# Two pairs of heads to a PSUM bank in half of the value products, some scores a slot later, left-over queries in other banks, and keys transposed without zeros

## The chip, the cores and the metric

The program runs on one core of one Trainium2 chip. The metric is the device time of one execution in microseconds, lower is better; the median of the runs is quoted. All matrix work is on TensorE (PE), with VectorE (DVE), ScalarE (ACT) and GpSimd (POOL) around it; SyncE (SP) issues the DMAs.

## What is computed

```python
# q, k, v: (8 batches, 8 heads, 576 tokens, 64)
k_p = k.reshape(B, H, 72, 8, D).mean(axis=3)      # keys and values pooled by 8
v_p = v.reshape(B, H, 72, 8, D).mean(axis=3)
attn = softmax(q @ k_p.T / 8)                     # 72 keys per head
x = (attn @ v_p) -> rows of 512                   # 4608 x 512
# first MLP
h = x @ w_in                                      # 512 -> 1024
solu = h * softmax(h); ln = layernorm(solu) * g_ln
x = ln @ w_out                                    # 1024 -> 512
# second MLP
out = ((x @ w1) * (x @ w2)) @ w3 @ w_out2
```

## The kernel before

The program has three stages. In the first (0 to about 565 us of the trace) attention and the first MLP run together, in the second (to about 690 us) the MLP goes on while the weights of the second MLP are prepared, and the third is the second MLP alone. The change touches only the first stage.

**Groups and units.** The tokens of a batch are cut into two groups of the attention: the even group has 256 tokens (two tiles of 128), the odd one has 256 and the 64 left over, as a third tile `t = 2`. There are 16 groups `a` (names carry the number: `sc8_1_0` are scores of group 8, tile 1, first four heads). The first MLP works on units of 256 rows, one behind the attention by two groups.

**The order.** PE and SP execute in the order in which the code is written, and the code is driven by a table of slots: `put(slot, fn)` hangs a step on a slot, and each slot ends with a piece of the first MLP, either a quarter of 128 rows through `w_in` (kind h: six matmuls `h` of 512 columns) or a quarter of a column block through `w_out` (kind x or y: twelve matmuls `x` of 256 columns). A unit has 16 slots: hhhh xxxx hhhh yyyy. ACT, DVE and POOL are put in order by a list scheduler when the program is built, each engine then executes its list strictly in that order.

**Attention by steps** (`Group`): `pq` transposes 128 queries (four 128x128 transposes, ACT copies them to `qT`); `sc` makes scores in two banks of four heads each; `exp` takes the maxima (`mx`, DVE) and eight exponentials (`ea`, ACT); `normalize` scales them (`sm` DVE, `pr` POOL); `pt` transposes the probabilities (and `px` those of the left-over keys); ACT and DVE split them into high and low words; `av` multiplies them with the pooled values, five matmuls for each of the four pairs of heads, and ACT (`xh`) and DVE (`xl`) split the result into the input of the MLP. In odd groups DVE also copies the 64 left-over rows (`X`). The distances of these steps in slots are in `GAPS`.

**Keys** (`Batch`): `pool_k` sums eight tokens on DVE (`kp`), ACT copies the sums into a tile `KBD` that has zeros for the other head of a pair, `transpose_k` transposes `KBD` (`pkm`) and a masked tile `KLB` of the left-over keys (`pkl`), and ACT and DVE copy both to `bdt`, which has the keys of a pair of heads side by side with zeros between. The first batch pools with matmuls instead (`pool_k_first`).

**Banks.** PSUM has eight banks: three of tag `ba` (function `bank`) for the attention, three of tag `bm` (`bankm`) for `px`, `lt` (transposes of the normalised rows) and the outputs of `w_out`, two as one pair for `h`. A new tile must wait until the last reader of the bank's tile before it has read it.

**SP.** `store` sends the first MLP's output (`xo`, copied by ACT) to DRAM; that issue waits for `xo`, and the loads behind it on SP wait with it.

Of the kernel before, what the change touches and what calls it, by code (L numbers as in the profile page):

```python
# [18 lines left out]
def attention_moe_kernel(  # L19
# [25 lines left out]
    nc = tc.nc  # L45
# [218 lines left out]
    nc.gpsimd.memset(KBD, 0.0)  # L264
# [6 lines left out]
    KLB = A1.tile([P, H, D], F32, tag="KLB", name="KLB")  # L271
    nc.gpsimd.memset(QL, 0.0)
    nc.gpsimd.memset(KLB, 0.0)
# [12 lines left out]
    class Batch:  # L286


        def __init__(self, b):
            self.b = b  # L290
            self.k, self.v = [None, None], [None, None]

        def load_main(self, src, to, i):
            t = A.tile([P, 2, POOL * D], F32, tag="kvn", name=f"kv{self.b}_{i}")
            for hh in range(2):
                nc.sync.dma_start(
                    t[64 * hh : 64 * hh + 64],
                    src[self.b, 4 * i + hh : 4 * i + hh + 3 : 2, 0:512, :].rearrange("h (k e) d -> k h (e d)", e=POOL),
                )
            to[i] = t  # L300

        def load_left(self, src, copies):
            t = A.tile([P, POOL * D], F32, tag="kvl", name=f"kvl{self.b}", bufs=1)
# [4 lines left out]
            return t  # L308

        def load_k(self, i):  # L310
            self.load_main(k, self.k, i)

        def load_kl(self):
            self.kl = self.load_left(k, 1)

        def load_v(self, i):
            self.load_main(v, self.v, i)

        def load_vl(self):
            self.vn = self.load_left(v, 2)  # L320

        def pool_k(self, i):
            kp = A.tile([P, 2, D], F32, tag="kp", name=f"kp{self.b}_{i}", bufs=1)
            nc.vector.tensor_reduce(kp, self.k[i].rearrange("p c (e d) -> p c d e", e=POOL), axis=AX.X, op=ALU.add)
            for hh in range(2):
                r = slice(64 * hh, 64 * hh + 64)
                nc.scalar.activation(KBD[r, 2 * i : 2 * i + 2, hh, :], kp[r], AF.Copy)

        def pool_k_first(self, i):

            if i == 0:
                self.pm = bank(f"pkm{self.b}")
                self.bdt = A.tile([P, NP, 2, KP], F32, tag="bdt", name=f"bdt{self.b}")
                nc.gpsimd.memset(self.bdt, 0.0)
            for c in range(2):
                for a in range(2):
                    r, o = slice(D * a, D * a + D), (2 * i + c) * P + D * a
                    for e in range(POOL):
                        s_ = self.k[i][:, c, e * D : e * D + D]
                        nc.tensor.matmul(  # L340
                            self.pm[r, o : o + D], s_, ident[:, r], start=(e == 0), stop=(e == POOL - 1)
                        )

        def pool_kl(self):
            tree(self.kl[0:64], D)
            nc.gpsimd.tensor_tensor(KLB[0:64], heads(self.kl[0:64, 0:D], 64), head_mask(64), ALU.mult)

        def transpose_k(self):
            if self.b == 0:
                bdt, pm = self.bdt, self.pm.rearrange("p (c a k) -> p c a k", c=NP, a=2)  # L350
                for a in range(2):
                    r = slice(D * a, D * a + D)
                    nc.scalar.activation(bdt[r, :, a, 0:KM], pm[r, :, a, :], AF.Copy)
            else:
                bdt = self.bdt = A.tile([P, NP, 2, KP], F32, tag="bdt", name=f"bdt{self.b}")
                pm = bank(f"pkm{self.b}")
                for p in range(NP):
                    nc.tensor.transpose(pm[:, p * P : p * P + P], KBD[:, p].rearrange("p a d -> p (a d)"), ident)
                nc.scalar.activation(bdt[:, :, :, 0:KM], pm.rearrange("p (c a k) -> p c a k", c=NP, a=2), AF.Copy)
            pl = bank(f"pkl{self.b}")  # L360
            for p in range(NP):
                nc.tensor.transpose(
                    pl[:, p * P : p * P + P], KLB[:, 2 * p : 2 * p + 2].rearrange("p a d -> p (a d)"), ident
                )

            def left():
                for p in range(NP):
                    nc.vector.tensor_copy(
                        bdt[:, p, :, KM:KP],
                        pl[:, p * P + 16 * p : p * P + 16 * p + 16].rearrange("p (a k) -> p a k", a=2),  # L370
# [24 lines left out]
    class Group:  # L395
# [20 lines left out]
        def pq(self, t):  # L416
            n, nm = P, f"{self.a}_{t}"
            pq = bank("pq" + nm)
# [102 lines left out]
        def av(self, i):  # L521
# [4 lines left out]
            for p in (2 * i, 2 * i + 1):  # L526
                av = bank(f"av{self.a}_{p}")
# [10 lines left out]
                for i, (l, r) in enumerate(terms):  # L538
                    nc.tensor.matmul(av[:, 0:w], l, r, start=(i == 0), stop=(i == 4))  # L539
                split(x[0][:, p], x[1][:, p], av[:, 0:U])  # L540
                if self.g == 1:
# [98 lines left out]
    GAPS = [(1, 2, 4, 3)] + [(1, 3, 2, 5)] * (2 * B - 1)  # L640
# [24 lines left out]
    for a in range(NG):  # L665
# [399 lines left out]
```

## Time and profile before

| | us |
|---|---|
| median of 3 runs | 1323.86 |
| fastest of the runs | 1323.69 |
| the profiled execution | 1323.81 |
| its span, first to last instruction | 1322.0 |
| PE busy | 1239.4 (94%) |
| DVE busy | 825.8 (62%) |
| ACT busy | 534.0 (40%) |
| POOL busy | 422.6 (32%) |

The profiled execution stands within 0.05 us of the median, so times of the trace and of the runs can be set side by side; 1.81 us lie around the span. A busy PE is not PE at its peak, since matmuls are pipelined; what PE waits for is read from the rows that name a releaser. The rows that matter come below.

### The profile page before, as it was taken

To read this page: it belongs to the slowest core of one execution; us is meant where nothing else is said; L and a number is where in the kernel's file an instruction comes from. 1 tells how busy PE (TensorE), PEld (TensorE's weight loads), DVE (VectorE), ACT (ScalarE), POOL (GpSimd) and SP (SyncE) were. 2 spreads that over 40 slices of the span, in tenths; PEclk is the share of its full clock that TensorE was granted. 3 is DMA by queue.
4 is the path that set the end of the run, shared out by engine and by line. 5 is a ranking of instruction groups with operands and counts; after the bars stand their busy time and mean duration, and the time that the engine had idled before them with its cause. 6 is when DMAs were issued, how large, how long until landed. Compare 5 with 4: busy or idle time off the path is not lost.

```text
span 1322.0 us, 21967 instructions
## 1 busy us (share of the span) xinstructions
PE 1239.4 (94%) x8284; PEld 1125.3 (85%) x8284; DVE 825.8 (62%) x1629; ACT 534.0 (40%) x1515; POOL 422.6 (32%) x509
## 2 busy tenths in 40 slices
PE   7778989989998999999999999999999999999992
PEld 5467889888888888998988899999999999999992
DVE  6889877677777777645357555546454645454541
ACT  4565656666665656554354221212121212121210
POOL 4452534342524434220000141524243333334220
PEclk9889999999999999999999999999999999999997
DMA  9533536454544364313133101010101101010000
GB/s 230 140 104 101 153 98 164 116 160 128 159 112 118 116 160 120 100 59 136 39 113 126 32 2 64 1 64 1 65 31 35 58 7 65 1 64 1 33 1 32
DMA packets 85698, 109.43 MB, mean 83 GB/s; under 512 B 43608, under 2 KB 43608, under 8 KB 85592
## 3 DMA queue, kind: packets, MB, share of 16 engines
q1 hardware_dynamic: 85592, 108.03, 28.7%
q8 instruction: 65, 1.06, 0.3%
q14 instruction: 41, 0.34, 0.1%
HBM read 78.65 MB, written 29.36 MB: 82 GB/s over the span
## 4 chain that ended last, share of the span: by engine, by line
PE 74%; DVE 11%; DMA 6%; ACT 4%; issue 3%; SPq 1%; POOL 0%; ACTq 0%; DVEq 0%; POOLq 0%
PE p L925 9%; PE p L927 9%; PE p L926 9%; PE h L567 8%; PE acc L971 5%; PE acc L974 5%; PE acc L973 5%; DMA f<-in_moe_w_dram 4%; PE x L625 4%; PE x L624 4%; PE x L626 4%; PE av L539 2%; PE lt L610 2%; PE sc L436 2%; DVE cvb L180 1%
## 5 line engine op out<-in xcount | busy, mean ns | idle before, releaser
L945 POOL TENSOR_TENSOR a<-a,b 128x256 f32<-128x256 f32 x72 | 52.9, 735 | 477.5 <-DVE b L944 350.9
L929 ACT ACTIVATE p<-p 128x256 f32<-128x256 f32 x72 | 27.9, 387 | 397.6 <-PE p L927 365.7
L624 PE MATMUL x<-lnh,gwh 128*128 128x256 f32 x576 | 167.3, 290 | 0.0
L625 PE MATMUL x<-lnl,gwh 128*128 128x256 f32 x576 | 163.8, 284 | 2.6 <-DVE lnl L614 2.6
L626 PE MATMUL x<-lnh,gwl 128*128 128x256 f32 x576 | 163.4, 284 | 0.0
L189 POOL TENSOR_TENSOR cvb<-cvb,cvm 128x512 f32<-128x512 f32 x46 | 60.0, 1305 | 180.7 <-DVE cvm L182 148.6
L625 PEld LDWEIGHTS x<-lnl,gwh 128*128 128x128 f32 x576 | 110.8, 192 | 4.2 <-DVE lnl L614 3.2
L457 ACT ACTIVATE ea<-sc,mx 128x72 f32<-128x72 f32 x320 | 98.3, 329 | 36.9 <-DVE mx L454 36.8
L974 PE MATMUL acc<-wfl,ph 128*128 128x512 f32 x288 | 113.1, 393 | 0.0
L973 PE MATMUL acc<-wfh,ph 128*128 128x512 f32 x288 | 112.9, 392 | 0.0
L624 PEld LDWEIGHTS x<-lnh,gwh 128*128 128x128 f32 x576 | 110.6, 192 | 1.2 <-DVE lnl L614 0.2
L626 PEld LDWEIGHTS x<-lnh,gwl 128*128 128x128 f32 x576 | 110.6, 192 | 0.0
L944 DVE TENSOR_TENSOR b<-b,p 128x256 f32<-128x256 f32 x72 | 30.2, 419 | 122.9 <-PE p L927 122.9
L567 PE MATMUL h<-winh,xh 128*128 128x512 f32 x288 | 100.4, 430 | 0.0
L567 PE MATMUL h<-winl,xh 128*128 128x512 f32 x288 | 91.4, 399 | 0.0
L567 PE MATMUL h<-winh,xl 128*128 128x512 f32 x288 | 90.4, 395 | 0.0
L925 PE MATMUL p<-th,w1h 128*128 128x256 f32 x288 | 81.6, 283 | 1.1 <-ACT p L929 1.1
L971 PE MATMUL acc<-wfh,pl 128*128 128x512 f32 x288 | 82.5, 393 | 0.0
L614 DVE TENSOR_TENSOR lnl<-lt,lnh 128x512 fp32r<-128x512 f32 x72 | 49.2, 686 | 52.7 <-ACT lnh L613 52.1
L926 PE MATMUL p<-th,w1h 128*128 128x256 f32 x288 | 81.5, 283 | 0.0
L927 PE MATMUL p<-th,w1l 128*128 128x256 f32 x288 | 81.5, 283 | 0.0
L933 DVE TENSOR_TENSOR u<-p,p 128x256 f32<-128x256 f32 x72 | 30.3, 422 | 77.3 <-PE p L927 76.2
(196 smaller groups left out, 3766.9 us busy)
## 6 DMA issues: line engine op xcount, KB each, us to landing
f<-in_moe_w_dram SPq DMA_DIRECT2D x32, 512.0 KB, 6.2
x2d<-xo SPq DMA_DIRECT2D x36, 256.0 KB, 2.0
xq<-x2d SPq DMA_DIRECT2D x36, 256.0 KB, 2.7
out_dram<-ot SPq DMA_DIRECT2D x36, 256.0 KB, 2.5
kv<-in_k_dram SPq DMA_DIRECT2D x32, 256.0 KB, 3.6
q<-in_q_dram SPq DMA_DIRECT2D x32, 256.0 KB, 8.3
kv<-in_v_dram SPq DMA_DIRECT2D x32, 256.0 KB, 3.7
f<-in_moe_w_out_dram SPq DMA_DIRECT2D x16, 512.0 KB, 6.1
```

The costliest lines, as they stand in the source:

```text
L189: self.engine.tensor_tensor(self.f, self.f, self.m.bitcast(F32), ALU.add)
L457: nc.scalar.activation(e[0:n, x], half[a][:, h], AF.Exp, bias=mx[0:n, x : x + 1], scale=1.0, accum_out=sm[0:n, x : x + 1],)
L567: nc.tensor.matmul(self.ph[:, a], s_[:, c], w_[:, c, a * 512 : a * 512 + 512], start=first, stop=last)
L624: nc.tensor.matmul(o, gw[0][:, f, ws], self.th[:, f], start=(f == 0), stop=False)
L625: nc.tensor.matmul(o, gw[0][:, f, ws], self.tl[:, f], start=False, stop=False)
L626: nc.tensor.matmul(o, gw[1][:, f, ws], self.th[:, f], start=False, stop=(f == FC - 1))
L925: nc.tensor.matmul(o, wh[:, c, fsl], th[:, c], start=c == 0, stop=False)
L926: nc.tensor.matmul(o, wh[:, c, fsl], tl[:, c], start=False, stop=False)
L927: nc.tensor.matmul(o, wl[:, c, fsl], th[:, c], start=False, stop=c == 1)
L971: nc.tensor.matmul(accs[t], pl[:, ts], wh, start=False, stop=(fc == FC - 1))
L973: nc.tensor.matmul(accs[t], ph[:, ts], wh, start=(fc == 0), stop=False)
L974: nc.tensor.matmul(accs[t], ph[:, ts], wl, start=False, stop=False)
```

## The change

1. Value products of an even group: two pairs of heads go into the two halves of one bank, so a group takes two banks and not four, and ACT and DVE split 512 columns at a time, not 256. Odd groups (320 columns a pair) stay as they were.
2. The scores of tile 1 of an even group (from group 2 on) are put one slot later, and the gap from its `pt` to `av` is one slot shorter, so `av` stays where it was.
3. The transposed left-over queries (`pq` of tile 2) take a bank of tag `bm`, not `ba`.
4. Keys are loaded so that the two heads of a pair lie side by side. The pooled tile `kp` (now two buffers) is transposed as it is, two transposes a batch and not four, and ACT copies the two halves to two `bdt` tiles that are set to zero once. `KBD` and its copies on ACT are gone. The left-over keys are summed twice into one tile `KL8` (four POOL additions, no multiplication by the mask), one transpose and not four, and two DVE copies and not four. The first batch's pooling has 32 matmuls of 128 columns, not 64 of 64 columns.

```diff
-    KBD = A1.tile([P, NP, 2, D], F32, tag="KBD", name="KBD")
+    BDT = [A1.tile([P, NP, 2, KP], F32, tag=f"bdt{i}", name=f"bdt{i}") for i in range(2)]
...
+    KL8 = A1.tile([P, POOL * D], F32, tag="KL8", name="KL8")
...
         def load_k(self, i):
-            self.load_main(k, self.k, i)
+
+            self.load_main(k, self.k, i, lambda h, r: slice(h + 2 * r, h + 2 * r + 2))
...
         def pool_k(self, i):
-            kp = A.tile([P, 2, D], F32, tag="kp", name=f"kp{self.b}_{i}", bufs=1)
+            kp = self.kp[i] = A.tile([P, 2, D], F32, tag="kp", name=f"kp{self.b}_{i}")
             nc.vector.tensor_reduce(kp, self.k[i].rearrange("p c (e d) -> p c d e", e=POOL), axis=AX.X, op=ALU.add)
-            for hh in range(2):
-                r = slice(64 * hh, 64 * hh + 64)
-                nc.scalar.activation(KBD[r, 2 * i : 2 * i + 2, hh, :], kp[r], AF.Copy)
...
         def transpose_k(self):
...
+            if self.b:
+                self.pm = bank(f"pkm{self.b}")
+                for i in range(2):
+                    nc.tensor.transpose(
+                        self.pm[:, i * P : i * P + P], self.kp[i].rearrange("p a d -> p (a d)"), ident
+                    )
...
+            pl = bank(f"pkl{self.b}")[:, 0:P]
+            nc.tensor.transpose(pl, KL8[:, 2 * D : 4 * D], ident)
+            pl = pl[:, 0:64]
+            for a in range(2):
+                r = slice(D * a, D * a + D)
+                nc.scalar.activation(bdt[r, :, a, 0:KM], pm[r], AF.Copy)
...
-            pq = bank("pq" + nm)
+            pq = (bank if t < 2 else bankm)("pq" + nm)
...
             for p in (2 * i, 2 * i + 1):
-                av = bank(f"av{self.a}_{p}")
+                if self.g or p % 2 == 0:
+                    av_bank = bank(f"av{self.a}_{p}")
+                av = av_bank if self.g else av_bank[:, p % 2 * U : p % 2 * U + U]
...
-                split(x[0][:, p], x[1][:, p], av[:, 0:U])
-                if self.g == 1:
+                for n, (l, r) in enumerate(terms):
+                    nc.tensor.matmul(av[:, 0:w], l, r, start=(n == 0), stop=(n == 4))
+                if self.g == 0 and p % 2:
+                    ps = slice(p - 1, p + 1)
+                    split(x[0][:, ps], x[1][:, ps], av_bank.rearrange("p (c n) -> p c n", c=2))
+                elif self.g == 1:
+                    split(x[0][:, p], x[1][:, p], av[:, 0:U])
...
-    GAPS = [(1, 2, 4, 3)] + [(1, 3, 2, 5)] * (2 * B - 1)
+    GAPS = [(1, 2, 4, 3)] + [(1, 3, 2, 5 - (a % 2 == 0)) for a in range(1, 2 * B)]
...
-            put(base + 2 + 4 * t, grp.sc, t)
+            put(base + 2 + 4 * t + (a > 0 and a % 2 == 0 and t == 1), grp.sc, t)
```

Three places show what moves. The first is on PE after the value products of group 7 (`av7_3` is their last pair), where the scores of group 8, tile 1 (`sc8_1_0`, `sc8_1_1`) stand; `x2_5_1` is an output block of the first MLP. Before:

```order
L539 MATMUL av7_3_3397<-ptx7_3029,vlh3_2646 128x320
L539 MATMUL av7_3_3397<-ptx7_3029,VLL_111 128x320
L436 MATMUL sc8_1_0_3412<-bdt4_3183,qT8_1_3344 128x144 x2
L436 MATMUL sc8_1_1_3415<-bdt4_3183,qT8_1_3344 128x144 x2
L624 MATMUL x2_5_1_3421<-lnh5_3080,gwh_103 128x256
L625 MATMUL x2_5_1_3421<-lnl5_3081,gwh_103 128x256
```

and now, where twelve `x` matmuls stand between `av7_3` and these rows:

```order
L634 MATMUL x2_5_1_3305<-lnl5_2978,gwh_103 128x256
L635 MATMUL x2_5_1_3305<-lnh5_2977,gwl_104 128x256
L440 MATMUL sc8_1_0_3321<-bdt0_105,qT8_1_3234 128x144 x2
L440 MATMUL sc8_1_1_3324<-bdt0_105,qT8_1_3234 128x144 x2
L633 MATMUL x2_5_1_3305<-lnh5_2977,gwh_103 128x256
L634 MATMUL x2_5_1_3305<-lnl5_2978,gwh_103 128x256
```

The scores moved behind one slot of `x`. In the built program the bank of `av7_3`, which nothing needed for long before, is then the next one taken: by `pt8_0`, one slot of `x` after the scores.

The second place is DVE's list around the value products of group 8 (`xl8` splits them, `kp5_0` pools keys of batch 5, `mx9_0` are maxima of group 9; `cvm` and `cvb` belong to the conversion of a weight). Before:

```order
L180 SCALAR_TENSOR_TENSOR cvb_3778<-f64_3647,cvb_3778 128x512
L324 TENSOR_REDUCE kp5_0_3803<-kv5_0_3684 128x128
L101 TENSOR_TENSOR xl8_3667<-av8_0_3668,xh8_3666 128x256
L101 TENSOR_TENSOR xl8_3667<-av8_1_3676,xh8_3666 128x256
L181 TENSOR_SCALAR cvm_3777<-cvb_3778 128x512
L182 SCALAR_TENSOR_TENSOR cvm_3777<-f64_3647,cvm_3777 128x512
L101 TENSOR_TENSOR xl8_3667<-av8_2_3704,xh8_3666 128x256
L101 TENSOR_TENSOR xl8_3667<-av8_3_3712,xh8_3666 128x256
L454 TENSOR_REDUCE mx9_0_3740<-sc9_0_0_3723 128x4
L454 TENSOR_REDUCE mx9_0_3740<-sc9_0_1_3726 128x4
```

and now:

```order
L329 TENSOR_REDUCE kp5_0_3686<-kv5_0_3571 128x128
L101 TENSOR_TENSOR xl8_3557<-av8_0_3558,xh8_3556 128x512
L180 SCALAR_TENSOR_TENSOR cvb_3661<-f64_3537,cvb_3661 128x512
L181 TENSOR_SCALAR cvm_3660<-cvb_3661 128x512
L182 SCALAR_TENSOR_TENSOR cvm_3660<-f64_3537,cvm_3660 128x512
L458 TENSOR_REDUCE mx9_0_3623<-sc9_0_0_3606 128x4
L101 TENSOR_TENSOR xl8_3557<-av8_2_3590,xh8_3556 128x512
L458 TENSOR_REDUCE mx9_0_3623<-sc9_0_1_3609 128x4
```

The split of the first two pairs is one instruction, still behind `kp5_0`, and one step of the conversion (L180) stands behind it and not ahead; the first maxima come ahead of the second split. On ACT the two copies to `KBD`, which stood between the splits of `av8_1` and the copy `xo6_0`, are gone.

The third place is on PE after the odd group's left-over queries: `lt7_0_0`, the first transpose of the next normalised rows, 24 `x` matmuls after them, with the semaphores that each row waits for. Before:

```order
L626 MATMUL x2_6_1_3812<-lnh6_3515,gwl_104 128x256
L610 MATMUL lt7_0_0_3917<-ident_66,e7_0_3608 128x128 x4
L436 MATMUL sc9_2_0_3932<-bdt4_3183,qT9_2_3879 128x144 [waits DVE_49,Activation_49]
L436 MATMUL sc9_2_0_3932<-bdt4_3183,qT9_2_3879 128x144
L436 MATMUL sc9_2_1_3935<-bdt4_3183,qT9_2_3879 128x144 [waits PE_49]
```

and now:

```order
L635 MATMUL x2_6_1_3693<-lnh6_3405,gwl_104 128x256
L619 MATMUL lt7_0_0_3796<-ident_66,e7_0_3498 128x128 [waits Activation_49]
L619 MATMUL lt7_0_0_3796<-ident_66,e7_0_3498 128x128 x3
L440 MATMUL sc9_2_0_3811<-bdt0_105,qT9_2_3760 128x144 [waits DVE_49]
L440 MATMUL sc9_2_0_3811<-bdt0_105,qT9_2_3760 128x144
```

`lt7_0_0` now waits for ACT, since it takes the bank out of which ACT copies the left-over queries (`qT9_2`); the scores behind it need not wait for that any more. It is so in all odd groups but the first.

## Rows read from the trace of the kernel before

**Rows 1.** Windows: length; busy PE, PEld, DVE, ACT, POOL; PEclk, DMA share, GB/s.

```profile
0.00:135.00 135.00, 104.84 (x602) 82.36 (x603) 114.09 (x224) 71.28 (x237) 56.34 (x78) 0.91 0.59 146
135.00:565.00 430.00, 405.71 (x2767) 371.33 (x2766) 321.86 (x632) 269.06 (x911) 170.07 (x219) 0.99 0.48 130
```

**Rows 2.** Waits of PE, whole span: us in total, times, longest us.

```profile
PE av L539 <- DVE xl L101: 8.4, 5, 1.8
PE sc L436 <- DVE X L543: 7.4, 6, 1.4
...
PE pq L421 <- ACT ea L457: 6.2, 5, 2.2
...
PE sc L436 <- DVE xl L101: 2.2, 6, 0.4
```

**Rows 3.** Timeline of PE around the scores of an even group: start, us.

```profile
310.29 0.65 PE L436 MATMUL sc<-bdt,qT 128*128 128x144 f32 x4
312.05 0.73 PE L436 MATMUL sc<-bdt,qT 128*128 128x144 f32 x4 [1.11 <-DVE X L543]
...
315.49 0.60 PE L502 MATMUL pt<-ident,pr 128*128 128x128 f32 x4
```

**Rows 4.** Timeline of DVE there: the copies out of the third and fourth pair.

```profile
311.69 0.21 DVE L543 COPY X<-av 128x64 f32<-128x64 f32 x1
...
314.77 0.21 DVE L543 COPY X<-av 128x64 f32<-128x64 f32 x1
```

**Rows 5.** Timeline of PE around an even group's value products.

```profile
334.09 0.28 PE L539 MATMUL av<-pth,VBDh 128*128 128x256 f32 x1
...
337.89 0.76 PE L436 MATMUL sc<-bdt,qT 128*128 128x144 f32 x4 [0.37 <-DVE xl L101]
```

**Rows 6.** Timeline of DVE there.

```profile
326.90 0.69 DVE L614 TENSOR_TENSOR lnl<-lt,lnh 128x512 fp32r<-128x512 f32 x1
...
333.08 0.84 DVE L180 SCALAR_TENSOR_TENSOR cvb<-f,cvb 128x512 int32<-128x512 int32 x1
...
335.70 0.74 DVE L101 TENSOR_TENSOR xl<-av,xh 128x256 fp32r<-128x256 f32 x2
...
338.68 0.46 DVE L454 TENSOR_REDUCE mx<-sc 128x4 f32<-128x288 f32 x1 [0.15 <-PE sc L436]
```

**Rows 7.** Timeline of ACT there.

```profile
332.83 0.64 ACT L100 ACTIVATE xh<-av 128x256 fp32r<-128x256 f32 x2
335.81 0.63 ACT L327 ACTIVATE KBD<-kp 64x128 f32<-64x128 f32 x2 [2.34 <-DVE kp L324]
336.47 0.60 ACT L633 ACTIVATE xo<-x 128x512 f32<-128x512 f32 x1
```

**Rows 8.** Timeline of SP there: the store of xo, ahead of further loads.

```profile
337.09 0.33 SPq L634 DMA_DIRECT2D x2d<-xo  x1
```

**Rows 9.** Timeline of DVE in the following odd group.

```profile
342.24 2.00 DVE L324 TENSOR_REDUCE kp<-kv 128x128 f32<-128x1024 f32 x1 [0.70 <-DMA kv<-in_k_dram]
344.62 1.23 DVE L575 TENSOR_REDUCE ST<-h 128x1 f32<-128x1024 f32 x1 [0.39 <-PE h L567]
```

**Rows 10.** Timeline of ACT: a late weight, and the copy of the left-over queries.

```profile
277.56 0.68 ACT L170 ACTIVATE cvm<-f 128x512 f32<-128x512 f32 x1 [3.00 <-DMA f<-in_moe_w_dram]
...
351.89 0.61 ACT L424 ACTIVATE qT<-pq 128x512 f32<-128x512 f32 x1
```

**Rows 11.** Timeline of PE in an odd group: first transpose of rows, scores, transposes of keys.

```profile
352.13 0.60 PE L610 MATMUL lt<-ident,e 128*128 128x128 f32 x4
352.56 1.25 PE L436 MATMUL sc<-bdt,qT 128*128 128x144 f32 x8
...
359.66 0.60 PE L358 MATMUL pkm<-ident,KBD 128*128 128x128 f32 x4
...
360.45 0.71 PE L567 MATMUL h<-winh,xh 128*128 128x512 f32 x2
```

**Rows 12.** Timeline of PE: pooling of the first batch's keys.

```profile
6.10 9.29 PE L340 MATMUL pkm<-ident,kv 128*64 128x64 f32 x128 [6.10 <-DMA kv<-in_k_dram]
```

More of the change, by code (lines that the diff above doesn't have):

```diff
@@ L270, in attention_moe_kernel @@
     QL = A1.tile([P, H, D], F32, tag="QL", name="QL")
[L271 removed]
     nc.gpsimd.memset(QL, 0.0)
[L273 removed]
+    KL8 = A1.tile([P, POOL * D], F32, tag="KL8", name="KL8")
+    nc.gpsimd.memset(KL8[64:P, 2 * D : 4 * D], 0.0)
     def heads(t, n):
@@ L290, in __init__, with load_main, load_left @@
             self.b = b
[L291 to L293 removed]
+            self.k, self.v, self.kp = [None, None], [None, None], [None, None]
+            self.bdt = BDT[b % 2]
+        def load_main(self, src, to, i, heads_of):
             t = A.tile([P, 2, POOL * D], F32, tag="kvn", name=f"kv{self.b}_{i}")
[L295 removed]
+            for r in range(2):
                 nc.sync.dma_start(
[L297 to L298 removed]
+                    t[64 * r : 64 * r + 64],
+                    src[self.b, heads_of(4 * i, r), 0:512, :].rearrange("h (k e) d -> k h (e d)", e=POOL),
                 )
             to[i] = t
[L302 to L303 removed]
+        def load_left(self, t, src, copies):
             for c in range(copies):
@@ L332, in pool_k_first @@
                 self.pm = bank(f"pkm{self.b}")
[L333 to L342, printed above, removed]
@@ L344, in pool_kl @@
-        def pool_kl(self):
-            tree(self.kl[0:64], D)
-            nc.gpsimd.tensor_tensor(KLB[0:64], heads(self.kl[0:64, 0:D], 64), head_mask(64), ALU.mult)
-        def transpose_k(self):
-            if self.b == 0:
-                bdt, pm = self.bdt, self.pm.rearrange("p (c a k) -> p c a k", c=NP, a=2)
+            for a in range(2):
+                for e in range(POOL):
+                    nc.tensor.matmul(
+                        self.pm[D * a : D * a + D, i * P : i * P + P],
+                        self.k[i][:, a, e * D : e * D + D],
+                        ident,
+                        start=(e == 0),
+                        stop=(e == POOL - 1),
+                    )
@@ new lines, in pool_kl, with left @@
+        def pool_kl(self):
+            t = KL8[0:64]
+            for w in (4, 2):
+                nc.gpsimd.tensor_tensor(t[:, 0 : w * D], t[:, 0 : w * D], t[:, w * D : 2 * w * D], ALU.add)
+            for c in (2, 3):
+                nc.gpsimd.tensor_tensor(t[:, c * D : c * D + D], t[:, 0:D], t[:, D : 2 * D], ALU.add)
+        def transpose_k(self):
+            if self.b:
[3 more added lines that the diff above has]
+                        self.pm[:, i * P : i * P + P], self.kp[i].rearrange("p a d -> p (a d)"), ident
+                    )
+            bdt, pm = self.bdt, self.pm[:, 0 : NP * KM].rearrange("p (c k) -> p c k", c=NP)
+            pl = bank(f"pkl{self.b}")[:, 0:P]
+            nc.tensor.transpose(pl, KL8[:, 2 * D : 4 * D], ident)
+            pl = pl[:, 0:64]
+            for a in range(2):
+                r = slice(D * a, D * a + D)
+                nc.scalar.activation(bdt[r, :, a, 0:KM], pm[r], AF.Copy)
+            def left():
@@ L351, in transpose_k @@
                 for a in range(2):
                     r = slice(D * a, D * a + D)
[L353 to L367, printed above, removed]
                     nc.vector.tensor_copy(
-                        bdt[:, p, :, KM:KP],
-                        pl[:, p * P + 16 * p : p * P + 16 * p + 16].rearrange("p (a k) -> p a k", a=2),
+                        bdt[r, :, a, KM:KP], pl[r].rearrange("p (c a k) -> p c a k", c=NP, a=2)[:, :, a]
```

14 lines of the change are left out of this document (6 added, 8 removed).

## The prediction

> **What bounds the kernel now.** I read the windows first. In the first 135 us PE is busy for 105 us and DVE for 114: there the list of DVE (conversion of weights, attention) sets the pace, and PE waits for what comes out of it. From 135 to 565 us PE is busy for 405.7 of 430 us and DVE for 321.9, so PE sets the pace and 24.3 us of it are idle [rows 1]. Behind 565 us nothing is changed. Then I read what PE waits for: 8.4 us in value products and 2.2 us in scores for the split on DVE (`xl`), 7.4 us in scores for the copy of the left-over rows (`X`), 6.2 us in the transposes of left-over queries for the exponentials [rows 2]. All four are waits for a bank whose last reader is late, and the edits aim at just these: 24.2 us together. So the most that can come back from waits is known; the question is whether the late reader is passed by, or is met again at the next bank. For that I walk through one period of two groups, with the readers' times.
>
> **Scores a slot later (A).** Before, the second half of the scores starts at 312.05, after a wait of 1.11 us for the copy that starts at 311.69 and takes 0.21 [rows 3, 4]: 0.15 us from the reader's end to PE's start. With a slot of `x` ahead of the scores this bank is free in time. But the built program gives the bank of the odd group's fourth pair to the next `pt`, which PE now reaches at about the time when it formerly reached it less the wait, 315.49 - 1.11 = 314.38, and the copy out of that pair ends only at 314.98 [rows 3, 4]; nothing on DVE ahead of it is removed. So `pt` starts at 314.98 + 0.15 = 315.13, and the gain here is 0.36 us and not 1.11. The new wait would be shown at `pt`, some 0.7 us each, for DVE `X`.
>
> **Two pairs to a bank (B).** Two banks fewer are taken, so the fourth pair waits for nothing, and the next wait is that of the second half of the scores, which takes the bank of the first two pairs. PE without waits: a slot of 256-column matmuls costs 0.12 us each (24 of them and half of the scores lie between 312.05 and 315.49), so from 334.09 ten of them and half of the scores, about 0.5, lead to 335.8, less the 0.36 of step A: 335.4; before it was 337.89 [rows 3, 5]. DVE: the split of the pairs began at 335.70, behind the pooling of keys. One step of 0.84 us now stands behind it; a split of 512 columns out of PSUM takes 0.69 by the row of `lnl`, where two of 256 took 0.74 [rows 6]. Bounds: 335.70 - 0.84 + 0.69 + 0.15 = 335.7 if the whole step is saved, 336.5 if nothing is (the steps ahead wait for ACT anyway). I take 336.2, nearer to the second: PE is then 1.7 us ahead of before, with some 0.8 us still waited, now in scores for `xl`.
>
> The first split on ACT starts at 332.83 [rows 7], when the matmuls of both first pairs are through: holding it until the second pair is done costs nothing. The Trainium skill (PSUM — Partial Sum Buffer, "PSUM bank collisions raise a hardware error") says that two engines must not touch one bank and quarter of partitions at once, so the first pair cannot be drained while the second is written. By that rule each split could begin five matmuls later, 0.6 us, in seven groups 4.2 us less gain; the row above says that ACT comes later than that, so my sum has none of it, and I keep it as a small rival.
>
> **The odd group behind it (C).** DVE's list from the split to the first maxima has the same work, so those maxima end about where they ended before (339.1) although PE is 1.7 us ahead [rows 6]. Then come key pooling, which waited 0.70 us for its load, and the maximum of the MLP's rows (`ST`), which began at 344.62 after 0.39 us of waiting for PE [rows 9]. The load comes earlier now: the store of `xo` at 337.09 went ahead of it on SP, and `xo` stood on ACT behind the two copies to `KBD`, which had waited 2.34 us for the pooling [rows 7, 8]. With these copies gone, `xo` can run at about 334.4, when its block is done, some 2 us sooner, and the loads follow. So pooling starts at about 341.4 and `ST` at 343.4, 1.2 us sooner; from there DVE and ACT run as before to the copy of the left-over queries, which ended at 351.89 + 0.61 = 352.50 [rows 10] and now ends at 351.3. PE, 1.7 ahead, comes to `lt` at 352.13 - 1.7 = 350.4, and `lt` now needs the bank out of which this copy reads: it waits 0.9 us. The scores behind it, formerly at 352.56, start 0.43 us after `lt` [rows 11], at 351.7. **Net 0.85 us a period**, of 2.81 us of waits in it. Bounds: -0.4 (the copy as late as before) and 2.8 (nothing late). There are seven even groups behind the first: 7 x 0.85 = 6.0 us.
>
> **Left-over queries in other banks (D).** Where a weight came late, ACT waited up to 3.00 us ahead of its exponentials [rows 10], and this is what made the 6.2 us [rows 2]. Taking the transposes out of these banks alone gains nothing, since the copy stands behind the same exponentials on ACT, and `lt` waits for it. The earlier loads do: 2 us of lead against waits of at most 3. Bounds 0 and 6.2; I take 2.5, since part of the 6.2 lies in the first stretch, where DVE rules.
>
> **Transposes (E).** Eight transposes from 359.66 to 360.45: 0.099 us each [rows 11]. Five fewer in seven batches and three in the first are 38 x 0.099 = 3.8 us. They stand between matmuls on an engine that waits for nothing there, so I count them whole.
>
> **The start (F).** The first batch's pooling takes 9.29 us for 128 records, two for each of 64 matmuls, 0.145 us a matmul [rows 12]. 32 matmuls of twice the columns cost between 4.6 us (same time each) and 9.3 (twice). DVE sets the pace there [rows 1], so of up to 4.6 us little arrives; DVE itself loses few instructions, and its list is put in another order, which can cost as much. Bounds -4 and +4.6; I take 1.5.
>
> Moved or added work that I cost at nothing: POOL's sums of left-over keys and the zeros of two `bdt` tiles instead of one (POOL is busy for 170 of 430 us, and nothing on PE waits for it there [rows 1, 2]); SP issues the same DMAs in the same order; two ACT copies of half the partitions for one.
>
> **Sum.** 6.0 + 2.5 + 3.8 + 1.5 = 13.8 us from the profiled execution of 1323.81, which is also the median: **1310 us**.
>
> **Rivals.** *All waits go*: DVE and ACT are not late any more, since both lose work and the loads come sooner. Then 24.2 of waits, 3.8 and 1.5 come back: 1294. For it: DVE has 108 us to spare from 135 to 565 [rows 1], and shorter waits may be understated by the row, as PE starts up anew after each. Against: within the period DVE's list has no gap between 326.90 and 338.68 [rows 6]. I give it 0.15 (half of it below 1297.4).
> *The waits only move*: every late reader is met at the next bank (`pt`, scores, `lt`), C gives nothing and D nothing. Then 3.8 is left: 1320. Chance 0.22.
> *The bank rule binds*: 13.8 - 4.2 = 9.6, 1314. Chance 0.05.
> *Slower than before*: `lt` waits in seven odd groups for the queries' copy, which stands on ACT behind exponentials and late weights, where before only a bank of the attention waited. If ACT is late by the 3.00 us of [rows 10] in each, beyond what step C has, 7 x 3.0 = 21 us are lost against a gain of 13.8: 1331. It decides from about 2.0 us a group on. Against it speaks that the copies to `KBD` leave just this list. Chance 0.04.
> *It doesn't do what it says*: the order shown above has the moved rows, so I give this no chance of its own.
>
> **How the numbers follow.** The forecast has 0.54, from 1303 to 1316 (the bounds of B and F). To leave out no more than 2 in 10, the range takes in the lower rival's time and goes half way to the upper: 1299 to 1320. About 2% (26 us) is what a measurement of this kernel tells from no change: faster by more than that needs nearly all of the waits, 0.09; slower by more needs more than the slower case has, 0.01; the rest, 0.90, is within.
>
> **What the profile of the changed kernel would show.** A: the wait of scores for `X` is gone, and `pt` waits for `X`, some 0.7 us six times. B: no wait of `av` for `xl` in even groups, one of scores for `xl` of about 0.8. C: `lt` waits for ACT `qT` about 0.9 us in odd groups; `xo` runs right behind the first split, and the store 2 us earlier. D: `pq` waits for nothing. E: three transposes of keys a batch. PE's idle time from 135 to 565 us falls from 24 to some 16. Wrong would make it, above all, a DVE list that runs ahead of the split faster than I take it (then steps A to C give up to three times as much), or an order of the first 135 us that costs or gives more than 5 us.

## The result, and the profile after

The changed kernel takes **1300.22 us** (median of four runs, 1299.68 to 1301.00) against 1323.78 for the kernel before beside it. That is 23.6 us between the medians, where 13.8 were forecast: the time lies at the lower edge of the range, and below the forecast's own 1303 to 1316. The ratio of the two kernels, as estimated from the runs, is 0.9841, with a 95% interval from 0.9813 to 0.9869, which is 21.0 us (17 to 25). One run of the kernel before (1744.62 us), and below one of `a_xact` (4265.32), stand far above all others; the ratios leave them out, and they move the medians by less than 1 us.

In the three later sets of runs the kernel before had medians of 1320.96, 1320.47 and 1319.88, with single runs from 1314.57 to 1325.41; the changed kernel was timed only in the first set. Against all 41 of these later runs (median 1320.91) the gain is 20.7 us. Differences of some 3 us between kernels of different sets therefore decide nothing below.

The profiled execution took 1300.06 us, its span is 1298.3. The windows of the changed kernel, with the columns of [rows 1]:

```profile
0.00:135.00 135.00, 103.75 (x537) 81.19 (x537) 113.42 (x216) 70.74 (x229) 58.92 (x79) 0.90 0.58 147
135.00:565.00 430.00, 420.21 (x2897) 385.84 (x2896) 330.57 (x636) 273.67 (x915) 173.48 (x222) 1.00 0.48 133
```

From 135 to 565 us PE is idle for 9.8 us, not 24.3 [rows 1] (nor the 16 of the forecast). The end of this window is already work of the second stage; the work that filled it before now fills 133.7 to 539.4, with 10.1 us idle. What PE waits for now, over the whole span, to be set beside [rows 2]:

```profile
PE pt L506 <- POOL pr L481: 10.7, 6, 4.4
...
PE sc L440 <- ACT qT L428: 5.8, 4, 4.1
PE pt L506 <- DVE X L552: 5.6, 6, 1.0
PE lt L619 <- ACT qT L428: 3.0, 3, 2.0
PE sc L440 <- DVE X L552: 2.5, 1, 2.5
PE av L545 <- ACT ea L461: 2.3, 4, 1.6
PE x L634 <- DVE lnl L623: 1.9, 1, 1.9
```

Of the four waits that the edits aim at, three are gone: `av` and `sc` do not wait for `xl` any more, nor `pq` for the exponentials. The fourth, for `X`, is now a wait of `pt`, as step A had it, and once of `sc`.

The same period as in [rows 5 to 10], in the changed kernel. DVE:

```profile
314.60 0.69 DVE L623 TENSOR_TENSOR lnl<-lt,lnh 128x512 fp32r<-128x512 f32 x1 [1.14 <-ACT lnh L622]
315.20 0.68 DVE L517 TENSOR_TENSOR ptl<-pt,pth 128x512 fp32r<-128x512 f32 x1
...
316.24 1.23 DVE L584 TENSOR_REDUCE ST<-h 128x1 f32<-128x1024 f32 x1
317.50 0.43 DVE L173 TENSOR_SCALAR cvm<-cvm 128x512 f32<-128x512 f32 x1
...
321.78 2.02 DVE L329 TENSOR_REDUCE kp<-kv 128x128 f32<-128x1024 f32 x1
323.73 0.68 DVE L101 TENSOR_TENSOR xl<-av,xh 128x512 fp32r<-128x512 f32 x1
...
326.12 0.45 DVE L458 TENSOR_REDUCE mx<-sc 128x4 f32<-128x288 f32 x1
...
329.49 1.96 DVE L329 TENSOR_REDUCE kp<-kv 128x128 f32<-128x1024 f32 x1
331.38 1.23 DVE L584 TENSOR_REDUCE ST<-h 128x1 f32<-128x1024 f32 x1
```

ACT:

```profile
321.81 0.60 ACT L100 ACTIVATE xh<-av 128x512 fp32r<-128x512 f32 x1 [0.28 <-PE av L545]
323.23 0.60 ACT L642 ACTIVATE xo<-x 128x512 f32<-128x512 f32 x1 [0.83 <-PE x L635]
324.42 0.60 ACT L100 ACTIVATE xh<-av 128x512 fp32r<-128x512 f32 x1 [0.58 <-PE av L545]
...
338.47 0.65 ACT L428 ACTIVATE qT<-pq 128x512 f32<-128x512 f32 x1
```

SP:

```profile
323.86 0.33 SPq L643 DMA_DIRECT2D x2d<-xo  x1
```

and PE:

```profile
338.77 0.28 PE L635 MATMUL x<-lnh,gwl 128*128 128x256 f32 x1
339.17 0.66 PE L619 MATMUL lt<-ident,e 128*128 128x128 f32 x4
...
370.12 0.63 PE L506 MATMUL pt<-ident,pr 128*128 128x128 f32 x4 [0.93 <-DVE X L552]
```

To set these against the rows before, both are counted from the first `x` matmul of unit 6, at 326.75 us before and at 315.70 now. The second `kp` now begins 13.79 us behind it (before 15.49), the `ST` behind that 15.68 (17.87), the store 8.16 (10.34), and the copy of the left-over queries ends at 23.42 (25.75). `lt` starts 0.05 behind that, at 23.47. The `x` matmuls ahead of it follow each other at 0.12 us, so without the copy it would have started at 338.89 and not at 339.17: it still waits, for 0.28 us, though the list of waits does not name it (from the last matmul's end, 339.05, it is 0.12). `xl` begins at 8.03 and formerly at 8.95, the maxima at 10.42 and formerly 11.33: these two are what the walk did not have.

The gain can be followed along PE by the same x matmuls: their first stands at 111.4 us before and 110.6 now, the first of unit 14 at 599.4 and 574.2, the last one at 680.9 and 657.6. In between, the waits with a named releaser add up to 26.3 us before (24.5 of them ahead of unit 14) and to 12.1 now (9.7).

### The profile page after: what moved, and what is told of

The parts are those of the page before. It is cut to its first block, busy times and chain, and to the rows that moved or that the text cites. A ratio compares the mean times of both kernels' runs of the same rounds, so it can differ in the third digit from the quotient of the medians.

```text
span 1298.3 us, 21656 instructions
## 1 busy us (share of the span) xinstructions
PE 1228.6 (95%) x8182; PEld 1117.1 (86%) x8182; DVE 820.2 (63%) x1597; ACT 525.0 (40%) x1478; POOL 422.7 (33%) x509
## 3 DMA queue, kind: packets, MB, share of 16 engines
q8 instruction: 64, 1.05, 0.3%
## 4 chain that ended last, share of the span: by engine, by line
PE 68%; DVE 14%; DMA 7%; ACT 4%; issue 3%; POOL 2%; SPq 1%; POOLq 0%; DVEq 0%; ACTq 0%
PE p L934 9%; PE p L936 9%; PE p L935 9%; PE h L576 7%; PE acc L980 5%; PE acc L983 5%; PE acc L982 5%; DMA f<-in_moe_w_dram 4%; PE x L634 3%; PE x L633 3%; PE x L635 3%; DVE cvb L180 2%; PE av L545 2%; PE lt L619 2%; ACT ea L461 2%
## 5 line engine op out<-in xcount | busy, mean ns | idle before, releaser
L634 PEld LDWEIGHTS x<-lnl,gwh 128*128 128x128 f32 x576 | 110.7, 192 | 3.1 <-DVE lnl L623 2.1
L633 PEld LDWEIGHTS x<-lnh,gwh 128*128 128x128 f32 x576 | 110.6, 192 | 1.0 <-DVE lnl L623 0.2
L635 PEld LDWEIGHTS x<-lnh,gwl 128*128 128x128 f32 x576 | 110.7, 192 | 0.0
```

What stands on the lines that cost most here:

```text
L633: nc.tensor.matmul(o, gw[0][:, f, ws], self.th[:, f], start=(f == 0), stop=False)
L634: nc.tensor.matmul(o, gw[0][:, f, ws], self.tl[:, f], start=False, stop=False)
L635: nc.tensor.matmul(o, gw[1][:, f, ws], self.th[:, f], start=False, stop=(f == FC - 1))
```

## Experiments

All experiments were timed beside the kernel before. A to D are the letters of the prediction; the *keys* are point 4 of the change. For reading them I use one table, worked out from each kernel's timelines: the first `x` matmul of unit 0; PE's waits with a named releaser from there to unit 14, added up; and, as the mean of five periods (units 2, 4, 6, 8, 10), the time from the unit's first `x` matmul to the first `ST` of DVE, to the first `xl`, to the store of `xo`, and to the end of the copy of the left-over queries (`qT`).

| kernel | median us | first x | waits | ST | xl | store | qT ends |
|---|---|---|---|---|---|---|---|
| before | 1319.9 to 1323.8 | 111.4 | 24.5 | 1.52 | 9.69 | 11.07 | 27.63 |
| b_A: before, with A | 1313.44 | 110.7 | 20.3 | 0.54 | 8.42 | 9.81 | 26.09 |
| b_B: before, with B | 1331.29 | 115.7 | 28.5 | 1.42 | 9.64 | 11.03 | 26.45 |
| b_D: before, with D | 1322.81 | 111.9 | 26.3 | 1.56 | 9.73 | 11.11 | 27.23 |
| b_keys: before, with the keys | 1317.62 | 114.5 | 20.3 | 1.48 | 9.68 | 8.50 | 26.56 |
| a_noA: after, without A | 1307.65 | 112.2 | 18.0 | 1.85 | 10.08 | 8.77 | 25.09 |
| a_noB: after, without B | 1305.10 | 112.0 | 14.1 | 0.54 | 8.16 | 8.17 | 24.64 |
| a_noD: after, without D | 1301.36 | 111.4 | 9.9 | 0.54 | 8.20 | 8.16 | 23.77 |
| b_ABD: after, without the keys | 1318.45 | 114.0 | 23.7 | 0.54 | 8.30 | 9.69 | 25.88 |
| a_kbd: after, KBD copies on ACT | 1309.23 | 112.1 | 20.2 | 0.54 | 8.37 | 9.76 | 25.67 |
| b_ABDpool: b_ABD, copies on POOL | 1306.96 | 113.5 | 11.8 | 0.54 | 8.15 | 8.17 | 23.87 |
| a_tr5: after, 38 transposes more | 1304.75 | 111.0 | 9.4 | 0.54 | 8.15 | 8.16 | 23.29 |
| a_xact: after, X copied by ACT | 1298.24 | 108.9 | 10.9 | 0.54 | 8.06 | 8.17 | 23.86 |
| after | 1300.22 | 110.6 | 9.7 | 0.54 | 8.13 | 8.16 | 23.33 |

**One part at a time.** The first set takes the kernel before and makes one part of the change alone.

b_A:

```diff
-    GAPS = [(1, 2, 4, 3)] + [(1, 3, 2, 5)] * (2 * B - 1)
+    GAPS = [(1, 2, 4, 3)] + [(1, 3, 2, 5 - (a % 2 == 0)) for a in range(1, 2 * B)]
-            put(base + 2 + 4 * t, grp.sc, t)
+            put(base + 2 + 4 * t + (a > 0 and a % 2 == 0 and t == 1), grp.sc, t)
```

> The kernel before with the scores a slot later alone (step A). By the prediction's walk the wait of scores for DVE X goes, pt waits some 0.7 us for it instead, and 6 x 0.36 = 2.2 us come back: 1321.6 us. If each edit returns its own wait whole, the 7.4 us of that wait come back: 1316.4. In both the long waits of av for xl (1.3 to 1.8 us each) stay, and so do the stretches at half clock behind two of them, near 408 and 480 us.

1313.44 us, ratio 0.9950 (0.9933 to 0.9967), a gain of 7.5 us. The waits in its profile:

```profile
PE pt L502 <- DVE X L543: 6.1, 6, 1.1
PE sc L436 <- DVE xl L101: 5.9, 7, 1.2
...
PE av L539 <- DVE xl L101: 4.1, 6, 1.9
```

So the wait for `X` did move to `pt`, six times, as the walk has it, and yet 7.5 us came back. That is the number of the theory by which its own wait comes back whole, but not its way. A place that the walk did not look at has moved: `xl` begins 1.27 us sooner on the mean (the table's 9.69 and 8.42), and the wait of `av` for it is halved. This alone is not the gain, since the wait of `sc` for `xl` grew from 2.2 to 5.9 us, so that PE waits for `xl` 10.0 us in all, and 10.6 before. By the table the waits of all names are 4.2 us less and the start is 0.7 us sooner; one stretch at the lower clock (the last section) fewer is 1.7 us.

b_B:

```diff
-                av = bank(f"av{self.a}_{p}")
+                if self.g or p % 2 == 0:
+                    av_bank = bank(f"av{self.a}_{p}")
+                av = av_bank if self.g else av_bank[:, p % 2 * U : p % 2 * U + U]
...
```

> The kernel before with two pairs of heads to a bank in the even groups alone (step B). By the walk PE comes out of the value products 1.3 us sooner, but DVE and ACT do not, so PE meets them again in the odd group: at most 2 us in all, 1322 us. If the waits are returned whole, 8.4 us of av and some of the 2.2 of sc come back: 1313 to 1315. A third theory is that the fall of the granted clock to 0.57 to 0.61 behind the long waits of av is part of the price: then the two stretches near 408 and 480 us run at 1.00 as well, some 4 us more on top of whatever waits come back.

1331.29 us, ratio 1.0079 (1.0057 to 1.0101): a loss of 10.3 us. The wait of `av` is gone, and others took its place:

```profile
PE pq L421 <- ACT ea L457: 12.5, 7, 3.5
PE sc L436 <- DVE X L548: 10.6, 7, 2.5
...
PE sc L436 <- DVE xl L101: 4.7, 5, 1.1
```

`pq` waits 12.5 us, not 6.2 [rows 2]; the waits are 4.0 us more in all, and the first 110 us take 4.3 us longer, in another order of the lists. No theory had the loss; of the three, the walk is the nearest.

b_D:

```diff
-            pq = bank("pq" + nm)
+            pq = (bank if t < 2 else bankm)("pq" + nm)
```

> The kernel before with the left-over queries' transposes in the other set of banks alone (step D). By the walk nothing comes back, since the copy of the queries still stands behind the same exponentials on ACT and the next transpose of the MLP waits for it: 1323.8, with waits of lt for qT where pq waited. If the waits are returned whole, the 6.2 us of pq come back: 1317.6, and one stretch at half clock near 138 us besides.

1322.81 us, ratio 1.0010 (0.9991 to 1.0028), nothing: what `pq` waited for (6.2 us) `lt` now does (5.7 us, five times, up to 2.2). The walk was right.

b_keys has point 4 of the change as it stands and nothing else:

```diff
-            for hh in range(2):
-                r = slice(64 * hh, 64 * hh + 64)
-                nc.scalar.activation(KBD[r, 2 * i : 2 * i + 2, hh, :], kp[r], AF.Copy)
...
-                    nc.tensor.transpose(pm[:, p * P : p * P + P], KBD[:, p].rearrange("p a d -> p (a d)"), ident)
```

> The kernel before with the new way of the keys alone (no zeros in the transposes, no KBD copies, wide matmuls in the first batch). By the walk 3.8 us of transposes and 1.5 at the start come back, and the loads start some 2 us earlier, which takes part of the 6.2 us of pq: 1316 to 1318.5. If the loads decide nothing here, 1318.5 with the waits of pq as before. If the key copies are what makes DVE and ACT late at the split, the waits of av for xl shrink by more than 4 us in all and the time is under 1314.

1317.62 us, ratio 0.9976 (0.9955 to 0.9996), 3.3 us. The time is in the walk's range, but that was counted from 1323.8, and the kernel before beside it took 1320.96: the walk had a gain of 5.3 to 7.8. The 1.5 us at the start did not come (the first `x` is 3.1 us later). The store of `xo` is 2.6 us sooner, but `xl` is where it was, and `av` waits 8.8 us for it.

The four gains are 7.5, -10.3, -1.9 and 3.3: together -1.4, against 21 to 24 when all are made. So the gain lies in the parts working together, and I went on by taking one part out.

**One part taken out.** The edits are made in the changed kernel, and the differences given are between medians. The changed kernel was timed in another set; by the ratios to the kernel before beside each, the same differences are 9.4 us (a_noA), 7.4 (a_noB), 18.1 (b_ABD), 2.9 (a_noD), 10.7 (a_kbd) and 6.3 (a_tr5), each good to some 5 us. a_noA:

```diff
-    GAPS = [(1, 2, 4, 3)] + [(1, 3, 2, 5 - (a % 2 == 0)) for a in range(1, 2 * B)]
+    GAPS = [(1, 2, 4, 3)] + [(1, 3, 2, 5)] * (2 * B - 1)
...
-                put(base + 2 + 4 * t + (a > 0 and a % 2 == 0 and t == 1), grp.sc, t)
+                put(base + 2 + 4 * t, grp.sc, t)
```

> The changed kernel with the scores in their old slot and the old gaps (step A taken back). One theory adds the single edits up (A alone gave 7.5 us, B alone lost 10.3, D alone lost 1.9, the keys alone gave 3.3): then 1300.2 + 7.5 = 1308. The other holds that the waits are passed on and vanish only when every bank's late reader is passed by: without A the second half of the scores waits for X again (1.1 to 1.4 us six or seven times) and for xl (about 1.05 us in six even groups, as with B alone), some 14 us: 1314.

1307.65 us, ratio 0.9912 (0.9882 to 0.9943): 7.4 us more than the changed kernel, which is the sum's number, but the waits are those of the other theory: `sc` for `X` 10.3 us in seven groups, and for `xl` 5.1 us in five. DVE in the period of unit 6, which begins at 322.4 here:

```profile
323.17 0.43 DVE L173 TENSOR_SCALAR cvm<-cvm 128x512 f32<-128x512 f32 x1 [2.08 <-ACT cvm L170]
...
324.70 1.21 DVE L584 TENSOR_REDUCE ST<-h 128x1 f32<-128x1024 f32 x1
...
332.91 0.67 DVE L101 TENSOR_TENSOR xl<-av,xh 128x512 fp32r<-128x512 f32 x1
```

and PE:

```profile
333.64 0.76 PE L440 MATMUL sc<-bdt,qT 128*128 128x144 f32 x4 [1.06 <-DVE xl L101]
```

Here stands what A does. Without it a conversion step (`cvm`), which waits for ACT, stands in DVE's list ahead of `ST`, and everything behind it comes late, the split too. So it was before the change, here in the period of unit 8, which begins at 394.94:

```profile
395.82 0.43 DVE L173 TENSOR_SCALAR cvm<-cvm 128x512 f32<-128x512 f32 x1 [2.20 <-ACT cvm L170]
...
397.35 1.21 DVE L575 TENSOR_REDUCE ST<-h 128x1 f32<-128x1024 f32 x1
```

With A `pt` is a slot later, the scheduler puts its `ptl` into that place and the conversion behind `ST` (L173 at 317.50 in the rows of the changed kernel). In all nine kernels with A `ST` begins 0.54 us into the period, in the five without it 1.4 to 1.9 on the mean. From `ST` to the pooling of keys DVE then takes 5.54 us in most periods with A, and 6.3 to 6.4 on the mean without it.

a_noB:

```diff
-                if self.g or p % 2 == 0:
-                    av_bank = bank(f"av{self.a}_{p}")
-                av = av_bank if self.g else av_bank[:, p % 2 * U : p % 2 * U + U]
+                av = bank(f"av{self.a}_{p}")
...
```

> The changed kernel with one pair of heads to a bank again (step B taken back). If the edits add up, B alone cost 10.3 us and this kernel is faster than the changed one: 1290. If the waits are passed on, the wait of av or of sc for xl returns as with A alone (1.3 to 1.9 us in six even groups, and a stretch at half clock behind some of them): 1308 to 1313.

1305.10 us, ratio 0.9897 (0.9865 to 0.9929): 4.9 us more. `av` waits for `xl` again, 2.9 us in six groups, and `sc` 3.1 us in seven. B alone is a loss, in company it is a gain; the waits come back smaller than I had them, since A has brought `xl` forward.

b_ABD takes out point 4 of the change as a whole, so that the copies, the transposes with zeros and the narrow first batch are back; of the edit these lines matter most:

```diff
+            for hh in range(2):
+                r = slice(64 * hh, 64 * hh + 64)
+                nc.scalar.activation(KBD[r, 2 * i : 2 * i + 2, hh, :], kp[r], AF.Copy)
...
```

> The changed kernel with the keys as before (KBD copies on ACT, transposes with zeros, narrow matmuls in the first batch): steps A, B and D without E, F and the earlier loads of C. If the edits add up 1321.0 - 7.5 + 10.3 + 1.9 = 1326 on the runs of before, 1325.7 and more. By the prediction's own terms for the keys alone (3.8 + 1.5) 1305.5. If the KBD copies are what makes the lists of ACT and DVE late (step C), 4 to 10 us more: 1310 to 1316, with waits of sc for xl, of lt for qT, or of pq and lt for ACT back in the profile.

1318.45 us, ratio 0.9978 (0.9958 to 0.9997): 18.2 us more, with A, B and D in it. Its longest wait:

```profile
PE lt L615 <- ACT qT L424: 15.7, 7, 3.9
```

This is the mechanism of the prediction's slower rival: in seven odd groups `lt` waits for the copy of the queries, 2.2 us on the mean and up to 3.9, the size that the rival had for each. The keys are what takes it away.

a_noD:

```diff
-            pq = (bank if t < 2 else bankm)("pq" + nm)
+            pq = bank("pq" + nm)
```

> The changed kernel with the left-over queries' transposes in the old banks (step D taken back). If the edits add up, D alone cost 1.9 us and this is 1298. If D removed a wait that the other edits do not reach, pq waits for ea again, 2 to 6 us in all: 1302 to 1306. If the earlier loads of step C had already taken that wait away, 1300 with lt waiting for nothing in the odd groups.

1301.36 us, ratio 0.9863 (0.9836 to 0.9890): not to be told from the changed kernel. `pq` waits 4.8 us in six groups and `lt` no more: the same wait under another name.

**What in the keys it is.** The last set takes them apart. a_kbd puts the copies to a tile that nobody reads back on ACT:

```diff
             nc.vector.tensor_reduce(kp, self.k[i].rearrange("p c (e d) -> p c d e", e=POOL), axis=AX.X, op=ALU.add)
+            for r in (slice(0, 64), slice(64, P)):
+                nc.scalar.activation(KBD[r, 2 * i : 2 * i + 2, 0, :], kp[r], AF.Copy)
...
```

> The changed kernel with the two copies of the pooled keys put back on ACT behind each pooling (into a tile that nobody reads), where they stood before: ahead of xo in the even groups. Transposes and the first batch stay new. If these copies are what the keys are worth (step C), most of the 18.2 us come back as a loss, 1311 to 1317, with the store of xo some 2 us later and lt waiting for qT in the odd groups. If the fewer transposes and the new first batch are, 1300 to 1303, since the copies themselves are 4 x 0.3 us a batch on an engine with time to spare. The prediction's own step C (6.0) gives 1306.

1309.23 us, ratio 0.9922 (0.9903 to 0.9941): 9.0 us more. Its wait of `lt`, to be held against the 3.0 us of the changed kernel:

```profile
PE lt L622 <- ACT qT L431: 13.1, 7, 2.6
```

and ACT in the period of unit 6, which begins at 321.85:

```profile
330.43 0.63 ACT L332 ACTIVATE KBD<-kp 64x128 f32<-64x128 f32 x2 [1.28 <-DVE kp L330]
331.08 0.60 ACT L645 ACTIVATE xo<-x 128x512 f32<-128x512 f32 x1
...
341.31 0.68 ACT L170 ACTIVATE cvm<-f 128x512 f32<-128x512 f32 x1 [1.63 <-DMA f<-in_moe_w_out_dram]
341.89 1.10 ACT L588 ACTIVATE e<-h,ST 128x1024 f32<-128x1024 f32 x1
```

The chain of step C and D, row by row: two copies of 0.63 us together wait 1.28 us for the pooling; `xo` behind them runs 9.23 us into the period, not 7.53; the store and the loads behind it on SP go out 1.7 us later; the weight `f` lands later and ACT, which waits 1.63 us for it, converts it at 19.46 and not 16.96 (the copies of the batch's second pooling stand ahead of it on ACT, but are done before it lands); the exponential behind it and in the end the queries' copy are 2.5 us later (25.9 and 23.4), and `lt` waits for that copy 2.3 us (at 347.82).

b_ABDpool leaves the transposes with zeros and moves only these copies:

```diff
-                nc.scalar.activation(KBD[r, 2 * i : 2 * i + 2, hh, :], kp[r], AF.Copy)
+                nc.gpsimd.tensor_copy(KBD[r, 2 * i : 2 * i + 2, hh, :], kp[r])
```

> Steps A, B and D with the keys as before, but with the copies to KBD on POOL in place of ACT: the transposes with zeros and the narrow first batch stay. If ACT's waiting for the pooled keys ahead of xo is the cause, the waits of lt for qT (15.7 us in seven groups) go without any change to the transposes: 1304 to 1307, that is the changed kernel and the 3.8 us of transposes and 1.5 at the start. If transposes and first batch are the cause, 1316 to 1320.

1306.96 us, ratio 0.9919 (0.9890 to 0.9949): 11.5 us less than b_ABD (7.8 by the ratios), by moving 28 small copies (four in each of seven batches) to another engine. `lt` waits 5.3 us, not 15.7, and the store is back at 8.17. What is left to the changed kernel is 6.7 us; by the traces it has in it a first `x` that is 2.9 us later and 2.3 us more of `lt`'s waits, besides the transposes.

a_tr5 adds transposes whose results are not read:

```diff
+            for c in range(1, 4):
+                nc.tensor.transpose(plb[:, c * P : c * P + P], KL8[:, 2 * D : 4 * D], ident)
+            if self.b:
+                for c in range(2, 4):
+                    nc.tensor.transpose(
+                        self.pm[:, c * P : c * P + P], self.kp[1].rearrange("p a d -> p (a d)"), ident
+                    )
...
```

> The changed kernel with the 38 key transposes of 128 columns added again (five in each batch, three in the first; their results are not read). Step E by itself: at 0.099 us each 3.8 us, 1304.0, if PE is what bounds there. Nothing, 1300, if PE waits at the next bank anyway; more than 6 us if PE's lateness is passed on to DVE and ACT.

1304.75 us (1301.19 to 1309.64), ratio 0.9889 (0.9861 to 0.9916): 4.5 us more, where 3.8 were counted. In the traces unit 0 to unit 14 take 2.6 us longer (466.2 and 463.6), and 30 of the 38 transposes lie there, 3.0 us as they were counted. The two agree with the count within what they can tell.

a_xact is the attempt at a faster kernel:

```diff
-                    nc.vector.tensor_copy(X8[bt.b // 4][:, p, c0 : c0 + TL], av[:, U : U + TL])
+                    nc.scalar.activation(X8[bt.b // 4][:, p, c0 : c0 + TL], av[:, U : U + TL], AF.Copy)
```

> The changed kernel with the four copies of the odd groups' left-over rows (X) on ACT in place of DVE: an attempt at a faster kernel, and a test of step A, by which the wait went from sc to pt and is set by DVE's list (split, copy, split, copy). If so, pt waits for less than 0.3 us in the six odd groups and some 4 us come back: 1296. If ACT then is late for the exponentials that stand behind the copies, it is no gain or a loss: 1300 to 1305.

1298.24 us, ratio 0.9835 (0.9818 to 0.9851): by ratio the same as the changed kernel. `pt` does not wait for `X` any more, and now `sc` does:

```profile
PE sc L440 <- ACT X L552: 5.9, 7, 0.9
```

The copies stand on ACT behind an `e` of 1.11 us. The wait has moved again, by one bank.

## Why the prediction was right, and where it was wrong

The direction, the order of size and most of the mechanism were right; the sum was 9.8 us short of the median beside it, some 7 of the median of the later runs. By its own steps:

- **A** said that the wait for `X` moves to `pt`, some 0.7 us six times. It is 5.6 us in six groups. But 0.36 us a group was its price, 2.2 us in all, and taking A out costs 7.4.
- **B** said 0.8 us of waiting of `sc` for `xl`. That is what a_noA shows (1.05 to 1.16 us in most even groups) and the changed kernel does not: the estimate was right for a DVE list that A had not changed. Holding the split until the second pair is done costs ACT 0.28 and 0.58 us of waiting in the rows above, and PE nothing. The Trainium skill's rule on a bank touched by two engines (PSUM — Partial Sum Buffer, "PSUM bank collisions raise a hardware error") thus had no price here; no run shows what it is to break it.
- **C** is the step that failed. It says: "DVE's list from the split to the first maxima has the same work, so those maxima end about where they ended before". The work is the same: 2.38 us from the first split to the first maximum before, 2.39 now, since a conversion step (L180) has come in and the second split has gone out. But the split itself begins 0.92 us sooner, and the first maximum 0.91. Of this 0.22 is an `ST` that comes sooner, and from there to the pooling DVE takes 5.54 us and not 6.33: L180 stands behind the split, where B had taken most of it as not saved, and the steps are shorter (L174 0.42 us, and 0.84 before). On the mean of the five periods the split is 1.56 us sooner, and 0.98 of it is `ST`: the *order* of the list, not its work, had put a waiting conversion ahead of it. From there C's walk runs as written, only ahead by that much: the second `kp` 1.70 us sooner (0.84 forecast; 0.9 of it are the maxima, 0.70 the wait for its load, which is gone), `ST` 2.19 (1.2), the queries' copy 2.33 (1.2). Counted from the `x` matmul, which A was to bring forward by 0.36, each of these forecasts is 0.36 less. So `lt`, forecast to wait 0.9 us in seven odd groups, waits in three by the list, 3.0 us in all (2.0 of it in the first); in two more it starts 0.2 to 0.3 us late, and in two not at all. The part of C that rests on `KBD`, `xo`, the store and the loads was right (the store 2.18 us sooner, 2 forecast), and a_kbd prices it at 9.0 us, where C and D had 8.5 for everything that comes of waits.
- **D** said that the banks alone gain nothing and the earlier loads do. Both shown: b_D and a_noD change nothing but the name of the waiting instruction, and a_kbd brings 13.1 us of that wait back.
- **E** was right (3.8 us forecast for 38 transposes; a_tr5 gives 4.5 for all, and 2.6 for 30 of them).
- **F** had 1.5 us. The first `x` stands 0.7 us sooner. The pooling of the first batch itself gave PE nothing: 32 matmuls of 128 columns take 9.06 us, 64 of 64 took 9.29 [rows 12], its upper bound. The rest is the order of the lists, and in the fourteen kernels this point lies anywhere from 108.9 to 115.7 us; b_keys is 3.1 us later than before.

In numbers: of the 23.3 us by which the last `x` matmul is sooner, 14.2 are named waits, where the sum had 8.5 (C and D); 3.0 are transposes (30 of the 38 lie behind the first `x`, at 0.099 us), 0.7 the start. A further 3.4 us were in no step: TensorE's granted clock, below. The remaining 2.0 us no row names. Waits cost PE somewhat more than the list says (1.33 us at 336.16 in the kernel before, where it started 1.48 us behind its pace of 0.12 us a matmul), and the changed kernel has ten waits fewer up to unit 14: by this estimate 1.5 us.

The rival *all waits go* (1294) missed by 6.2 us, my forecast by 9.8, so the result lies between the two and nearer to the rival. What it had over the forecast is the text's own last warning, that a DVE list which runs ahead of the split faster than assumed would give far more in steps A to C; I had this as a risk and not as a step, because I read from the built order what stood between split and maxima, and not what stood ahead of the split and of `ST`.

## What to carry to other kernels

Where PE runs in a fixed order and meets the readers of its banks, one edit alone can show little or a loss, since the wait is met at the next bank; follow the late reader's whole list back to the instruction in it that itself waits, not just to the bank. A cheap copy can be dear by what stands behind it: copies of 0.3 us, two of them ahead of an output copy, held a store and behind it the loads, and cost 9.0 us. When a step is moved in a list that a scheduler orders, compare the built lists of *all* engines around it, also where no work is added or taken away.

## What the hardware showed that I had not expected

PE's long waits can be paid twice. In the kernel before, PE waited 1.83 us for `xl` at 405.96; after that the granted clock was at the lower of its two levels (1.2 against 2.4 GHz) for a while:

```profile
404.00:408.00 4.00, 1.80 (x13) 1.46 (x12) 3.96 (x8) 1.77 (x5) 1.66 (x2) 1.00 0.09 30
408.00:412.00 4.00, 4.00 (x14) 3.25 (x13) 1.16 (x4) 2.54 (x16) 1.14 (x2) 0.57 0.57 164
```

The columns are those of [rows 1]: PE is busy for 1.80 of 4 us, then for all of 4 at 0.57 of the full clock. Before had three such stretches (behind waits of 2.18, 1.83 and 1.71 us), the changed kernel has one, behind a wait of 1.89 us at 602.10. Adding up (1 - granted clock) over slices of 2 us from 110 to 690 us gives 5.1 us before and 1.7 after; it came in steps of 1.7 in the others (b_A 3.4, b_ABD 8.5, a_noB none). The Trainium skill (TensorE: Matmul & The Clock Gate, "HAM oscillation — how this bites in real kernels") describes idle gaps, longer than these, that cost clock besides; the rows agree that they do, and show it for shorter ones. It does not follow each time: the 1.84 us at 265.94 in the kernel before had no such stretch behind it, nor the 2.03 us of `lt` at 140.10 in the changed kernel. Whether that is also why the 41 later runs of the kernel before spread over 10.8 us, and the four of the changed kernel over 1.3, stays open: the fastest and the slowest of the 41 have a mean granted clock of 0.981 and 0.979.

DVE's conversion step L174 took 0.43 us at 326.44 in the kernel before and 0.84 at 332.20, where POOL was summing the left-over keys (331.84 to 334.09). The Trainium skill (SBUF — State Buffer, "Who interferes with whom") has POOL and DVE share a port that one of them holds for a whole instruction. The rows fit that, but no experiment separated it.
